# One transformer layer: a fixed issue order for the first units, chunk 2 turned by DMA, earlier mask constants, a new plan search

## The chip, the cores and the metric

The kernel runs on one core of a Trainium2 chip. A core has a matmul engine (TensorE, called PE in the profile; its weight loads appear as PEld), a vector engine (VectorE, DVE), a scalar engine (ScalarE, ACT), a general engine (GpSimd, POOL) and a sync engine (SyncE, SP) that mostly issues transfers (DMAs). Each engine runs its own instructions in the order of the program; between engines, semaphores order the work. The time is device microseconds for one execution of the whole kernel, with the median over several runs.

## The reference

The input x has 2048 tokens of 448 features, in bf16. A conditioning row c gives six rows of modulation, and two branches follow, each with a layer norm in front:

```
mod = (silu(c) @ w_mod)                      # six rows: sa, ca, ga, sb, cb, gb
h = layernorm(x) * (1 + ca) + sa
x = x + ga * A(h)
h = layernorm(x) * (1 + cb) + sb
x = x + gb * B(h)
```

A is attention with 16 heads of 28. A token attends to 8 keys: itself and those 2, 4, ... 14 positions back (keys before the start are masked out); its output goes through wo. B is a layer norm followed by an MLP: `gelu(y @ w1 + b1) @ w2 + b2`, with 1792 inner features.

## The kernel before

**Tiling.** Even and odd tokens are stored apart, so that a window with dilation 2 becomes a contiguous window of 8 within 1024 tokens. The 2048 tokens are 16 blocks of 128 (b or t in the code). Four blocks make a chunk, so there are chunks 0 to 3.

**Stages.** `front_ln(bs)` does the first layer norm for a list of blocks: per block a bn_stats and bn_aggr on VectorE (`stats`, L621), the reciprocal deviation on ScalarE (`rstd_act`, L626, an Ln and an Exp) for chunks 0 and 1 or on GpSimd (`rstd_pool`, L636) for 2 and 3, then a normalized block z on VectorE (`normalize`, L645). Then z must be turned, so that the features lie on the partitions, and the modulation (scale and bias per feature) is applied, which gives hT. There are two ways. For chunks in `TURN_PE` (L29) the matmul engine turns z with an identity matrix into PSUM (L757), and VectorE (L772) and ScalarE (L776) evict it, half each, with the modulation in the same instruction. For the other chunks SP issues a DMA transpose per block straight into hT (L781), and four VectorE instructions apply the modulation in place (L785). `front_qk(bs)` makes q and k from hT on PE (L705 and L712; the name pq), and ScalarE copies them out (L821). `values(b)` makes v (pv), ScalarE copies it (L854) and a DMA moves part of it to other partitions (L857). Chunk 0 goes through `front_ln` and `front_qk` in two units of two blocks, [0, 1] and [2, 3]; the other chunks go whole.

`attention(b)` handles one of nine groups: scores on PE (lt, L925), exp on ScalarE (et, L935), the mask on VectorE (L943), sums and values on PE (pd L957, po L965), Ln and Exp of the sums on ScalarE (den), and the division on VectorE (L991). `out_proj(t)` multiplies with wo (pw, L1006), adds to x (L1010), does the second and third layer norms on VectorE and turns the result y by DMA into yT (L1032). `mlp(j)` does four blocks of the MLP: w1 products (L705, L712, the name p), gelu on ScalarE (L1063), w2 products (L1076), the final addition (L1084) and the store. These come in three phases: attention 0 to 4 and MLP tile 0; attention 5, 6 and tile 1; attention 7, 8 and tiles 2, 3. Work for chunks 1, 2 and 3 is added behind attention 0, 2 and 3.

**What sets the order.** The code does not issue anything directly: every step is a task given to a planner (`add`) with its engine, an assumed duration, what it reads and writes, and the buffers it needs. The planner simulates the engines, picks among ready tasks the one of the highest rank, and searches: it disturbs the ranks at random for `TURNS` turns, the first `WIDE` of them widely and with a backward pass that recomputes ranks from the schedule, and keeps the order with the lowest mean cost over `DRAWS` replays with randomly longer tasks (`SLOW`). Two things bind the search. `rank_add` raises a task's rank. `seq` gives tasks of one engine a fixed order among themselves (`keep_sequences`, L131). The rank at the start (L153) includes `rank_add`; a backward pass (L155) computes ranks without it. PE idle time before 12 us is filled with warm-up matmuls (dummy, L613; L615), in a number proportional to `FILL_SHARE`.

**Loads.** The first loads stand in one list on SP: x of blocks 0 and 1, the modulation weights (wm_st), q and k weights, x of 2 and 3, v weights, x of 4 to 7; then `load_early` brings x of 8 to 11, the other modulation weights, x of 12 to 15, wo and b2. GpSimd memsets wo's tile to zero first (L538), since wo is loaded into it with gaps. GpSimd tasks given through `pool` are either free at once (`gated=False`) or held behind a gate (`pool_late`, L566), which follows the spreading of the q and k weights (`spread`, L790, L799).

Of the kernel before, what the change touches and what calls it, by code (L numbers as in the profile page):

```python
# [25 lines left out]
LEAD, SEP = 8, 8  # L26
WQ, WK, WE = 57, 64, 58
HL, HTW = 64, 592
TURN_PE = (0, 1, 2)  # L29
VENG = "SP"  # L30
SBQ, NSB, NBT = 2 * WQ, 18, 9
SBE = 4 * WE
# [4 lines left out]
DEN_SCALE = 2.0 ** -32  # L37
EXP_SET = "natural_log_exp_and_others"
START, NOISE, WINDOW = 0.8, (0.3, 1.0, 3.0), 3.4133
SEED, TURNS, WIDE = 15, 1500, 60  # L40
QKG = {256: ((0,), (1,), (2,), (3,)), 512: ((0,), (1,), (2,), (3,))}
W1G = ((0,), (1,), (2,), (3,), (4,), (5,), (6,))
SPREAD = ("DVE", "DVE")
# [4 lines left out]
]  # L48
FRONTS = (0, 2, 3)
LMM, DMM = 0.59, 1.0  # L50
FILL_UNTIL, FILL_SHARE = 12.0, 1.0
ROOM = {"S": 8, "et": 2, "den": 2, "zh": 6, "zb": 5, "T": 4, "hm": 4, "vb": 3, "vs": 2, "xp": 6}
DMA_RATE, TR_BYTES = 340e3, 480e3
SWITCH, SAME = 0.095, 1.0
FLEX = ("F", "64x128")
SEM = 0.07
DRAWS = 6
SLOW = {"BW": (0.5, 2.0), "SP": (0.1, 0.0), "PE": (0.0, 0.0), "any": (0.08, 0.0)}
DRAIN = {"PE": 0.165, "DVE": 0.085, "ACT": 0.105, "POOL": 0.05, "SP": 0.0, "BW": 0.0}


# [24 lines left out]
class Planner:  # L86
# [60 lines left out]
    def ranks(self):  # L147
        for t in reversed(self.sorted_tasks()):
            tail = 0.0
            for a in t.after:  # L150
                lag = (DRAIN[t.eng] + SEM + t.late) if a.before[t] else 0.0
                tail = max(tail, a.rank + lag)
            t.rank = t.us + tail + t.rank_add  # L153

    def backward(self):  # L155

# [17 lines left out]
    def forward(self):  # L174
# [13 lines left out]
        while len(order) < len(self.tasks):  # L188
            started = False
            for e in ("PE", "DVE", "ACT", "POOL", "SP", "BW"):  # L190
                if free_at[e] > now:
                    continue
                best, best_key = None, None
                shared = e in port and port["DVE" if e == "POOL" else "POOL"] > now
                for t in ready[e]:
                    if ready_at[t] > now or (shared and t.port):
                        continue
                    key = (-ready_at[t], -t.n) if e == 'BW' else (t.rank + ((SAME if t.mode == mode or t.mode == "flex" and mode in FLEX else 0.5 * SAME if t.mode != "F" and mode not in FLEX else 0.0) if e == "PE" else 0.0), -t.n)
                    if best is not None and key < best_key:
                        continue  # L200
                    need = {}
                    for b in t.bufs:
                        if b.slot is None:
                            need[b.room] = need.get(b.room, 0) + 1
                    if all(sum(x <= now for x in room[r]) >= n for r, n in need.items()):
                        best, best_key = t, key
                if best is None:
                    continue
                t = best
                t.fill = 0  # L210
                if e == "PE" and now < FILL_UNTIL:
                    t.fill = int(max(0.0, now - free_at[e]) * FILL_SHARE / (0.43 if now < 6.8 else 0.215))
                ready[e].remove(t)
                order.append(t)
                t.start = now
                started = True
                for b in t.bufs:
                    if b.slot is None:
                        b.slot = min(range(ROOM[b.room]), key=lambda k: room[b.room][k])
                        room[b.room][b.slot] = 1e9  # L220
                end = now + t.us
                if e == "PE" and t.mode == "flex":
                    t.closing = mode != "F"
                    end += 0.0 if mode in FLEX else SWITCH
                    mode = "F" if t.closing else "64x128"
                elif e == "PE" and t.mode != mode:
                    end += SWITCH
                    mode = t.mode
                free_at[e] = end
                t.cost = end - now  # L230
                if t.port:
                    port[e] = end
                done = end + DRAIN[e] + t.late
                for b in t.bufs:
                    users_left[b] -= 1
                    if users_left[b] == 0:
                        room[b.room][b.slot] = done + SEM
                for a in t.after:
                    left[a] -= 1
                    at = done + SEM if a.before[t] else end  # L240
                    if a.eng == e == "PE" or (a.eng == e and not a.before[t]):
                        at = end
                    ready_at[a] = max(ready_at[a], at)
                    if left[a] == 0:
                        ready[a.eng].append(a)
            if started:
                continue
            times = [v for v in free_at.values() if v > now] + [v for r in room.values() for v in r if now < v < 1e9]
            times += [ready_at[t] for e in ready for t in ready[e] if ready_at[t] > now]
            if not times:  # L250
                return None, 1e9
            now = min(times)
# [125 lines left out]
def kernel(  # L378
# [156 lines left out]

    late_pool = []
    b2_bc = sb("zh", [128, D], BF16, "b2_bc")
    add("POOL", 1.6, lambda: nc.gpsimd.memset(wo_s[:], 0.0), writes=["wo"], rank_add=440)  # L538

    def early(fn, nbytes, writes, reads=(), bufs=()):  # L540
        t, u = dma("SP", 0.5, fn, nbytes, writes, reads, bufs, chain["head"])
# [14 lines left out]
    def load_mlp(behind):  # L556
        chain["behind"] = behind
        for kt in range(KT):
            bulk(lambda kt=kt: nc.sync.dma_start(out=w1_s[:, kt], in_=B_w1[KOFF[kt]:KOFF[kt] + 128]), F * 256, [f"w1{kt}"],
                 lambda kt=kt: w1_s[0:1, kt, 0:1])  # L560
        for i in range(4):
            f0, f1 = 4 * i, min(4 * i + 4, FT)
            bulk(lambda f0=f0, f1=f1: nc.sync.dma_start(
                out=w2_s[:, f0:f1], in_=B_w2[128 * f0:128 * f1].rearrange("(ft p) n -> p ft n", p=128)),
                (f1 - f0) * 256 * D, [f"w2l{f // 2}" for f in range(f0, f1, 2)], lambda f0=f0: w2_s[0:1, f0, 0:1])

    def pool_late():
        gate = add("POOL", 0.1, lambda: nc.gpsimd.memset(wqk_st.t[0:1, 1, KT - 1, D - 8:D], 0.0), bufs=[wqk_st],
# [21 lines left out]
    def mask_rows():  # L590
        nc.gpsimd.memset(mask1[:], 1.0)
        for j in range(2):
# [3 lines left out]
            nc.gpsimd.affine_select(out=m, in_=m, pattern=[[-1, WE]], compare_op=ALU.is_ge, fill=0.0,  # L596
                                    base=0, channel_multiplier=1)

    pool(0.8, mask_rows, ["mask1"])
    pool(0.9, lambda: nc.gpsimd.tensor_copy(out=mask[:], in_=mask1[:].unsqueeze(1).to_broadcast([128, 16, WE])), ["mask"],  # L600
         ["mask1"])

    def consts():
        for vk in vkeys:
# [1 line left out]
        nc.gpsimd.memset(ones_k[:], 1.0)  # L606
        nc.gpsimd.memset(ones_k[0:WIN - 1, 1, :], 0.0)

    pool(0.9, consts, ["ones", "vpad"])

    pwm = ps_one([128, 512], "pwm")

# [6 lines left out]


    def stats(src, key, sl, mv, b):  # L621
        first = mv is mv1 and b < 4
        add("DVE", 0.53, lambda: nc.vector.bn_stats(out=st_all[:, sl, :], in_=src()), reads=key, writes=[f"st{sl}"], seq=b + 20 * (b > 1) if first else None)  # L623
        return add("DVE", 0.09, lambda: nc.vector.bn_aggr(out=mv[:, b, :], in_=st_all[:, sl, :]), reads=[f"st{sl}"],
                   writes=[f"mv{id(mv)}_{b}"], seq=2 + b + 20 * (b > 1) if first else None)

    def rstd_act(mv, which, b0, n, ra=0.0):
        ks = [f"mv{id(mv)}_{b}" for b in range(b0, b0 + n)]
        add("ACT", 0.2, lambda: nc.scalar.activation(out=tv_all[:, which, b0:b0 + n], in_=mv[:, b0:b0 + n, 1],
                                                     func=ACT.Ln, bias=eps_col[:]),  # L630
            reads=ks + ["eps"], writes=[f"tv{which}_{b0}"], after=[tbl0], seq=3 if b0 == 0 else None)
        add("ACT", 0.15, lambda: nc.scalar.activation(out=rs_all[:, which, b0:b0 + n], in_=tv_all[:, which, b0:b0 + n],
                                                      func=ACT.Exp, scale=-0.5),
            reads=[f"tv{which}_{b0}"], writes=[f"rs{which}_{b}" for b in range(b0, b0 + n)], seq=4 if b0 == 0 else None)

    def rstd_pool(mv, which, b0, n):  # L636
        ks = [f"mv{id(mv)}_{b}" for b in range(b0, b0 + n)]
# [89 lines left out]
    def front_ln(bs):  # L727
        ch = bs[0] // 4
        early = ch in TURN_PE
        if ch not in h_of:  # L730
            h_of[ch] = sb("T", [128, KT, HTW], BF16, "hT")
        hc = h_of[ch]
        for b in bs:
            stats(lambda b=b: x_all[:, b, :], [f"x{b}"], b, mv1, b)
        if ch <= 1:
# [13 lines left out]
        if early:  # L749
# [15 lines left out]
            for half, eng in enumerate(("DVE", "ACT")):  # L765
                ptr = ptrs[half]
                for k in range(2):
# [3 lines left out]
                    if eng == "DVE":  # L771
                        add("DVE", 0.07 + n / 800, lambda kt=kt, k=k, ptr=ptr, scale=scale, bias=bias: nc.vector.tensor_scalar(  # L772
                            out=hc.t[:, kt, o:o + n], in0=ptr.t[:, k, :], scalar1=scale, scalar2=bias,
                            op0=ALU.mult, op1=ALU.add), reads=["sa", "ca"], writes=w, bufs=[ptr, hc], seq=12 + 2 * kt + 20 * (bs[0] > 1) if bs[0] < 4 else None)
                    else:
                        add("ACT", 0.32 + n / 1400, lambda kt=kt, k=k, ptr=ptr, scale=scale, bias=bias: nc.scalar.activation(  # L776
                            out=hc.t[:, kt, o:o + n], in_=ptr.t[:, k, :], func=ACT.Identity, scale=scale, bias=bias),
                            reads=["sa", "ca"], writes=w, bufs=[ptr, hc], seq=8 - kt if 0 in bs else None)
            return
        for b in bs:  # L780
            dma("SP", 1.25, lambda b=b: nc.sync.dma_start_transpose(out=hc.t[:, :, HL + b % 4 * 128:HL + b % 4 * 128 + 128], in_=zs[b].t[:]),  # L781
# [20 lines left out]
    def front_qk(bs):  # L802
# [3 lines left out]
        for mps in QKG[n]:  # L806
# [11 lines left out]
            for m, p in zip([2 * mp + i for mp in mps for i in range(2)], bufs):  # L818
                dst = (qT if m < 4 else kT)[:, m % 4, c0:c0 + n]
                w = [f"{'q' if m < 4 else 'k'}{m % 4}_{b}" for b in bs]  # L820
                add("ACT", 0.06 + n / 1200, lambda dst=dst, p=p: nc.scalar.copy(out=dst, in_=p.t[:]), bufs=[p], writes=w)  # L821

    def h_edges(ch):
        hc = h_of[ch]
# [354 lines left out]
```

## Time and profile before

| what | value |
|---|---|
| runs | 11, median 176.86 us, from 175.4 to 177.96 |
| profiled execution | 175.97 us, of which the span from first to last instruction is 174.3 us |
| first projection of q (L705, pq) starts | 9.92 us |
| first MLP product (p<-yT,w_s) starts | 69.5 us |
| last matmul ends | 171.34 us |
| transposes on PE (L757) | 48, from 6.45 to 37.6 us |
| DMA transposes for hT (L781) | 4, from 29.4 to 42.8 us |

A row of the timeline gives the start, the length, the engine, the line of the code, the operation, the result and what it is made of, the count of instructions merged in it, and in brackets the idle time ahead of it and what ended that. An engine with "q" behind its name is that engine's instruction queue, for example SPq issuing a transfer. Ends of matmuls are modelled by the profiler, so neighbouring rows can overlap by a few tenths. The weight tile w_s stands for w1 and w2, since the profile leaves numbers out.

### The profile page before, as it was taken

What the parts mean: (1) busy time and instruction counts of PE and PEld (TensorE: products, weight loads), DVE (VectorE), ACT (ScalarE), POOL (GpSimd) and SP (SyncE); (2) the same over time, 40 slices, a digit from 0 to 9 for tenths busy, and PEclk for the clock granted to TensorE, in tenths of its full rate; (3) what the DMA queues carried; (4) which work ended last, traced back from release to release, by engine and by line L of the source; (5) the groups of instructions that cost most, each with busy time, mean ns of one, the idle gap of its engine ahead of it and who ended that gap; (6) DMA issues with size and microseconds to landing.
All of it is one profiled execution on the core that took longest, in us unless ns stands there. A gap on an engine that the chain in (4) does not pass through costs nothing.

```text
span 174.3 us, 5056 instructions
## 1 busy us (share of the span) xinstructions
PE 165.8 (95%) x2093; PEld 82.4 (47%) x2110; DVE 116.5 (67%) x325; ACT 110.1 (63%) x199; POOL 46.6 (27%) x85
## 2 busy tenths in 40 slices
PE   7897999999999999999999999999999999999993
PEld 2464554554444545334555433555443555334562
DVE  2589957589999999993374899783779882001121
ACT  2158878899759988577867686956946400685000
POOL 5034004231382444161230233432213462000000
PEclk9999999999999999999999999999999999999999
DMA  5999983314199914004111100431001133000111
GB/s 150 271 361 270 259 167 115 62 29 98 26 335 257 268 38 90 2 4 92 30 56 34 30 4 0 90 88 56 0 4 32 25 88 83 4 0 0 53 53 53
DMA packets 22421, 16.01 MB, mean 92 GB/s; under 512 B 11961, under 2 KB 21182, under 8 KB 22398
## 3 DMA queue, kind: packets, MB, share of 16 engines
q1 hardware_dynamic: 22388, 15.69, 35.1%
q8 instruction: 16, 0.26, 0.6%
q14 instruction: 7, 0.06, 0.1%
q10 hardware_dynamic: 10, 0.00, 0.0%
HBM read 10.05 MB, written 1.84 MB: 68 GB/s over the span
## 4 chain that ended last, share of the span: by engine, by line
PE 88%; ACT 5%; DMA 3%; issue 1%; SPq 1%; DVE 0%
PE p L1076 25%; PE p L705 21%; PE pq L705 11%; PE pw L1006 7%; PE pv L705 6%; PE p L712 4%; DMA wm_st<-in_w_mod_dram 3%; PE pq L712 3%; PE po L965 3%; PE lt L925 3%; ACT et L935 2%; PE pd L957 1%; PE pv L712 1%; ACT hT L776 1%; ACT vkeys L854 1%
## 5 line engine op out<-in xcount | busy, mean ns | idle before, releaser
L1063 ACT ACTIVATE hm<-p,b_col 128x512 bf16<-128x512 f32 x56 | 35.1, 685 | 26.2 <-PE p L712 23.2
L1076 PE MATMUL p<-w_s,hm 128*128 128x448 bf16 (+1 forms) x238 | 44.1, 342 | 0.0
L705 PE MATMUL p<-yT,w_s 128*128 128x512 bf16 x160 | 39.2, 380 | 0.7 <-issue 0.5
L1084 DVE TENSOR_TENSOR x_all<-p,x1p 128x448 bf16<-128x448 f32 (+1 forms) x17 | 10.1, 596 | 34.8 <-PE p L1076 34.8
L641 POOL TENSOR_TENSOR rs_all<-tv_all,neg_half 128x1 f32<-128x1 f32 (+1 forms) x34 | 20.9, 631 | 41.5 <-DVE tv_all L638 41.4
L1076 PEld LDWEIGHTS <-hm 128*128 128x128 bf16 x238 | 22.7, 98 | 18.7 <-issue 0.2
L1036 POOL TENSOR_TENSOR x1p<-x_all,gbb_bc 128x448 f32<-128x448 bf16 x16 | 18.7, 1168 | 46.8 <-DVE x_all L1010 17.3
L705 PEld LDWEIGHTS <-w_s 128*128 128x128 bf16 x168 | 15.2, 98 | 21.8 <-issue 5.9
L705 PE MATMUL pq<-hT,Wqk 128*128 128x512 bf16 (+1 forms) x112 | 22.4, 334 | 2.2 <-issue 1.0
L623 DVE BATCH_NORM_STATS2 st_all<-x_all 128x6 f32<-128x448 bf16 x32 | 18.8, 614 | 5.0 <-DMA x_all<-in_A_x_dram 5.0
L935 ACT ACTIVATE et<-lt 128x464 bf16<-128x464 f32 x36 | 17.5, 571 | 1.9 <-PE lt L925 1.8
L705 PEld LDWEIGHTS <-Wqk 128*128 128x128 bf16 x120 | 10.9, 98 | 11.7 <-issue 2.8
L1006 PE MATMUL pw<-wo_s,oT 128*128 128x448 bf16 x64 | 14.1, 353 | 0.0
L943 DVE TENSOR_TENSOR et<-et,mask 128x928 bf16<-128x928 bf16 x18 | 13.1, 755 | 1.4 <-ACT et L935 1.4
L646 DVE TENSOR_SCALAR z<-x_all,mv,rs_all 128x512 bf16<-128x512 bf16 (+1 forms) x32 | 12.5, 418 | 1.7 <-POOL rs_all L641 1.7
L991 DVE TENSOR_TENSOR oT<-po,den 128x456 bf16<-128x456 f32 x18 | 10.8, 626 | 3.9 <-ACT den L981 3.9
L821 ACT CAST qT<-pq 128x512 bf16<-128x512 f32 (+1 forms) x20 | 9.2, 516 | 5.1 <-PE pq L712 3.5
L978 ACT ACTIVATE den<-pd 128x464 f32<-128x464 f32 x18 | 9.1, 562 | 5.1 <-PE pd L957 5.1
L1010 DVE TENSOR_TENSOR x_all<-pw,x_all 128x448 bf16<-128x448 f32 x16 | 9.9, 617 | 3.4 <-PE pw L1006 3.3
L705 PE MATMUL pv<-Wv,hT 128*128 128x448 bf16 x54 | 11.4, 353 | 0.0
L821 ACT CAST kT<-pq 128x512 bf16<-128x512 f32 (+1 forms) x20 | 9.1, 510 | 2.6 <-PE pq L712 2.0
L854 ACT CAST vkeys<-pv 128x448 bf16<-128x448 f32 x18 | 8.8, 534 | 1.7 <-PE pv L712 1.0
(87 smaller groups left out, 184.2 us busy)
## 6 DMA issues: line engine op xcount, KB each, us to landing
w_s<-in_B_w_dram SPq DMA_DIRECT2D x7, 448.0 KB, 4.2
wmod<-in_w_mod_dram SPq DMA_DIRECT2D x4, 392.0 KB
out_dram<-x_all SPq DMA_DIRECT2D x7, 224.0 KB, 2.3
x_all<-in_A_x_dram SPq DMA_DIRECT2D x3, 448.0 KB, 7.0
vb<-vkeys SPq DMA_DIRECT2D x9, 128.0 KB
wqk_st<-in_A_wqkv_dram SPq DMA_DIRECT2D x4, 226.0 KB
wm_st<-in_w_mod_dram SPq DMA_DIRECT2D x2, 392.0 KB, 5.9
x_all<-in_A_x_dram SPq DMA_DIRECT2D x2, 224.0 KB
```

The source lines that it names most:

```text
L623: add("DVE", 0.53, lambda: nc.vector.bn_stats(out=st_all[:, sl, :], in_=src()), reads=key, writes=[f"st{sl}"], seq=b + 20 * (b > 1) if fir ...
L641: lambda: nc.gpsimd.tensor_tensor(out=rs_all[:, which, b0:b0 + n], in0=tv_all[:, which, b0:b0 + n], in1=neg_half[:, 0:n], op=ALU.pow),
L646: return add("DVE", us, lambda: nc.vector.tensor_scalar(out=dst(), in0=src(), scalar1=mv[:, b, 0:1], scalar2=rs_all[:, which, b:b + 1], op ...
L705: nc.tensor.matmul(outs[i].t[:], lhsT=w(i, kt, slice(0, 128)), rhs=x(i, kt, slice(0, 128)), start=(n == 0 and not last), stop=(n == 2 and ...
L712: nc.tensor.matmul(outs[i].t[:], lhsT=w(i, kt, rows), rhs=x(i, kt, rows), start=not last, stop=last, tile_position=(r0, 0))
L821: add("ACT", 0.06 + n / 1200, lambda dst=dst, p=p: nc.scalar.copy(out=dst, in_=p.t[:]), bufs=[p], writes=w)
L935: ex = add("ACT", 0.45, lambda r=r: nc.scalar.activation(out=et.t[:, r].rearrange("p n ft c -> p (n ft c)"), in_=lts[r].t[:].rearrange("p ...
L943: nc.vector.tensor_tensor(out=ev, in0=ev, in1=mask[:], op=ALU.mult)
L1006: nc.tensor.matmul(pw.t[:], lhsT=oT[:, ft, c0:c0 + 128], rhs=wo_s[:, ft, :], start=(ft == 0), stop=(ft == 3))
L1036: P.wrote(add("POOL", 1.05, lambda: nc.gpsimd.tensor_tensor(out=xp.t[:], in0=x_all[:, t, :], in1=gbb2_bc[:], op=ALU.add), reads=[f"x{t}", ...
L1063: gl = add("ACT", 0.57, lambda f=f, p=p: nc.scalar.activation(out=hm_at(f), in_=p.t[:], func=ACT.Gelu_apprx_tanh, bias=b1_col[:, f:f + 1]) ...
L1076: nc.tensor.matmul(p2.t[:], lhsT=hm_at(f)[:, bi * 128:(bi + 1) * 128], rhs=w2_s[:, f, c0:c1], start=(f == 0), stop=(f == FT - 1))
```

## The change

It has five parts.

1. **Fixed order.** `stats` now gives the bn_stats of blocks 0 to 7, rather than 0 to 3, a place in VectorE's sequence; those of 4 to 7 get 34 to 37, behind the normalization of blocks 2 and 3 (30 and 31). The Ln and Exp of blocks 2 and 3 get places 13.5 and 13.6 on ScalarE, between the copies of q (10 to 13) and k (14 to 17) of blocks 0 and 1, which also get places. The VectorE eviction of the turned blocks 2 and 3 loses its place. All tasks of `front_ln([2, 3])` are raised by `BOOST`, 6.
2. **Turning.** `TURN_PE` is (0, 1), so that chunk 2 goes the way of chunk 3.
3. **GpSimd.** The mask, its copy and the constants are no longer gated and have high ranks; the memset of wo's tile becomes a gated task.
4. **Ranks.** `rank_add` no longer enters the stored rank (and with it that of the tasks in front); it is added when a ready task is picked, after a backward pass too.
5. **Search.** Another seed, 1400 turns with 400 wide ones for 1500 with 60, smaller assumed delays of transfers, and warm-up matmuls for 0.75 of the idle time.

```diff
-TURN_PE = (0, 1, 2)
+TURN_PE = (0, 1)
...
-SEED, TURNS, WIDE = 15, 1500, 60
+SEED, TURNS, WIDE = 3, 1400, 400
...
-FILL_UNTIL, FILL_SHARE = 12.0, 1.0
+FILL_UNTIL, FILL_SHARE = 12.0, 0.75
...
-SLOW = {"BW": (0.5, 2.0), "SP": (0.1, 0.0), "PE": (0.0, 0.0), "any": (0.08, 0.0)}
+BOOST = 6.0
+SLOW = {"BW": (0.3, 1.2), "SP": (0.1, 0.0), "PE": (0.0, 0.0), "any": (0.06, 0.0)}
...
-            t.rank = t.us + tail + t.rank_add
+            t.rank = t.us + tail
...
-                    key = ... else (t.rank + ((SAME if ...
+                    key = ... else (t.rank + t.rank_add + ((SAME if ...
...
-    add("POOL", 1.6, lambda: nc.gpsimd.memset(wo_s[:], 0.0), writes=["wo"], rank_add=440)
...
+    pool(1.6, lambda: nc.gpsimd.memset(wo_s[:], 0.0), ["wo"])
...
-    pool(0.8, mask_rows, ["mask1"])
+    pool(0.8, mask_rows, ["mask1"], gated=False, rank_add=700)
...
-         ["mask1"])
+         ["mask1"], gated=False, rank_add=690)
...
-    pool(0.9, consts, ["ones", "vpad"])
+    pool(0.9, consts, ["ones", "vpad"], gated=False, rank_add=680)
...
-        first = mv is mv1 and b < 4
-        add("DVE", 0.53, ... seq=b + 20 * (b > 1) if first else None)
+        first = mv is mv1 and b < 8
+        add("DVE", 0.53, ... seq=b + 20 * (b > 1) + 10 * (b > 3) if first else None)
         return add("DVE", 0.09, ...
-                   ... seq=2 + b + 20 * (b > 1) if first else None)
+                   ... seq=2 + b + 20 * (b > 1) if first and b < 4 else None)
...
-            (Ln) ... seq=3 if b0 == 0 else None)
+            (Ln) ... seq={0: 3, 2: 13.5}.get(b0) if which == 0 else None)
-            (Exp) ... seq=4 if b0 == 0 else None)
+            (Exp) ... seq={0: 4, 2: 13.6}.get(b0) if which == 0 else None)
...
-            (eviction of ptr on DVE) ... seq=12 + 2 * kt + 20 * (bs[0] > 1) if bs[0] < 4 else None)
+            (eviction of ptr on DVE) ... seq=12 + 2 * kt if 0 in bs else None)
...
+            if bs[0] == 2:
+                for t in P.tasks[n0:]:
+                    t.rank_add += BOOST
...
-                add("ACT", 0.06 + n / 1200, ... nc.scalar.copy(out=dst, in_=p.t[:]), bufs=[p], writes=w)
+                add("ACT", 0.06 + n / 1200, ... nc.scalar.copy(out=dst, in_=p.t[:]), bufs=[p], writes=w,
+                    seq=10 + m if 0 in bs else None)
```

More of the change, by code (lines that the diff above doesn't have):

```diff
@@ L197, in forward @@
                         continue
-                    key = (-ready_at[t], -t.n) if e == 'BW' else (t.rank + ((SAME if t.mode == mode or t.mode == "flex" and mode in FLEX else 0.5 * SAME if t.mode != "F" and mode not in FLEX else 0.0) if e == "PE" else 0.0), -t.n)
+                    key = (-ready_at[t], -t.n) if e == 'BW' else (t.rank + t.rank_add + ((SAME if t.mode == mode or t.mode == "flex" and mode in FLEX else 0.5 * SAME if t.mode != "F" and mode not in FLEX else 0.0) if e == "PE" else 0.0), -t.n)
                     if best is not None and key < best_key:
@@ L621, in stats @@
     def stats(src, key, sl, mv, b):
-        first = mv is mv1 and b < 4
-        add("DVE", 0.53, lambda: nc.vector.bn_stats(out=st_all[:, sl, :], in_=src()), reads=key, writes=[f"st{sl}"], seq=b + 20 * (b > 1) if first else None)
+        first = mv is mv1 and b < 8
+        add("DVE", 0.53, lambda: nc.vector.bn_stats(out=st_all[:, sl, :], in_=src()), reads=key, writes=[f"st{sl}"], seq=b + 20 * (b > 1) + 10 * (b > 3) if first else None)
         return add("DVE", 0.09, lambda: nc.vector.bn_aggr(out=mv[:, b, :], in_=st_all[:, sl, :]), reads=[f"st{sl}"],
-                   writes=[f"mv{id(mv)}_{b}"], seq=2 + b + 20 * (b > 1) if first else None)
+                   writes=[f"mv{id(mv)}_{b}"], seq=2 + b + 20 * (b > 1) if first and b < 4 else None)
     def rstd_act(mv, which, b0, n, ra=0.0):
@@ L630, in rstd_act @@
                                                      func=ACT.Ln, bias=eps_col[:]),
-            reads=ks + ["eps"], writes=[f"tv{which}_{b0}"], after=[tbl0], seq=3 if b0 == 0 else None)
+            reads=ks + ["eps"], writes=[f"tv{which}_{b0}"], after=[tbl0], seq={0: 3, 2: 13.5}.get(b0) if which == 0 else None)
         add("ACT", 0.15, lambda: nc.scalar.activation(out=rs_all[:, which, b0:b0 + n], in_=tv_all[:, which, b0:b0 + n],
                                                       func=ACT.Exp, scale=-0.5),
-            reads=[f"tv{which}_{b0}"], writes=[f"rs{which}_{b}" for b in range(b0, b0 + n)], seq=4 if b0 == 0 else None)
+            reads=[f"tv{which}_{b0}"], writes=[f"rs{which}_{b}" for b in range(b0, b0 + n)], seq={0: 4, 2: 13.6}.get(b0) if which == 0 else None)
     def rstd_pool(mv, which, b0, n):
@@ L732, in front_ln @@
         hc = h_of[ch]
+        n0 = len(P.tasks)
         for b in bs:
@@ L773, in front_ln @@
                             out=hc.t[:, kt, o:o + n], in0=ptr.t[:, k, :], scalar1=scale, scalar2=bias,
-                            op0=ALU.mult, op1=ALU.add), reads=["sa", "ca"], writes=w, bufs=[ptr, hc], seq=12 + 2 * kt + 20 * (bs[0] > 1) if bs[0] < 4 else None)
+                            op0=ALU.mult, op1=ALU.add), reads=["sa", "ca"], writes=w, bufs=[ptr, hc], seq=12 + 2 * kt if 0 in bs else None)
                     else:
@@ L820, in front_qk @@
                 w = [f"{'q' if m < 4 else 'k'}{m % 4}_{b}" for b in bs]
-                add("ACT", 0.06 + n / 1200, lambda dst=dst, p=p: nc.scalar.copy(out=dst, in_=p.t[:]), bufs=[p], writes=w)
+                add("ACT", 0.06 + n / 1200, lambda dst=dst, p=p: nc.scalar.copy(out=dst, in_=p.t[:]), bufs=[p], writes=w,
+                    seq=10 + m if 0 in bs else None)
     def h_edges(ch):
```

## The prediction

> **What bounds the kernel now.** I read the page's busy rows first, then the chain of waits, then the stages one by one.
>
> The first two sections of the page:
>
> ```profile
> span 174.3 us, 5056 instructions
> PE 165.8 (95%) x2093; PEld 82.4 (47%) x2110; DVE 116.5 (67%) x325; ACT 110.1 (63%) x199; POOL 46.6 (27%) x85
> ...
> PE   7897999999999999999999999999999999999993
> ...
> DVE  2589957589999999993374899783779882001121
> ACT  2158878899759988577867686956946400685000
> ...
> DMA  5999983314199914004111100431001133000111
> ```
>
> Each digit is 4.36 us. TensorE (PE) has 174.3 - 165.8 = 8.5 us of idle in the whole span, so no scheduling change can win more than that unless it also takes work off PE. The table by stages says where those 8.5 us lie (columns: length, then busy time and count of PE, PEld, DVE, ACT, POOL, then clock, DMA share, GB/s):
>
> ```profile
> 16.00:18.00 2.00, 0.87 (x9) 0.51 (x10) 2.00 (x9) 2.00 (x5) 0.00 (x0) 1.00 1.07 263
> ...
> 34.00:36.00 2.00, 1.95 (x34) 1.24 (x23) 0.50 (x1) 2.00 (x6) 0.00 (x0) 1.00 0.33 66
> 36.00:38.00 2.00, 1.93 (x16) 0.79 (x15) 2.00 (x4) 2.00 (x5) 1.31 (x1) 1.00 0.00 0
> 38.00:40.00 2.00, 1.61 (x124) 1.44 (x124) 2.00 (x6) 1.97 (x5) 0.00 (x0) 1.00 0.03 8
> ...
> 50.00:60.00 10.00, 9.79 (x238) 4.88 (x238) 9.73 (x30) 7.87 (x17) 3.68 (x6) 1.00 1.08 290
> 60.00:70.00 10.00, 9.74 (x125) 4.72 (x126) 9.86 (x29) 8.50 (x14) 5.14 (x7) 1.00 0.40 63
> ```
>
> About 3.0 us are the tail after the last matmul (the last matmul ends at 171.34; the last rows are then added and stored), 2.2 us are the start before 10 us, where the modulation weights are awaited, and no edit is aimed at either. What is left is one hole at 16 to 18 us (1.13 us), some 0.7 us at 34 to 42, and small gaps, most of them 0.16 us wherever the matmul shape switches. So I expect a gain of about one per cent at best, from the first 42 us. The hole at 16 us in the timeline (start, length, engine, line, result, count, wait):
>
> ```profile
> 13.50 1.68 DVE L623 BATCH_NORM_STATS2 st_all<-x_all 128x6 f32<-128x448 bf16 x3 [0.92 <-DMA x_all<-in_A_x_dram]
> ...
> 15.18 0.70 DVE L646 TENSOR_SCALAR z<-x_all,mv,rs_all 128x512 bf16<-128x512 bf16 x2
> ...
> 15.62 0.83 PE L757 MATMUL ptr<-ident,z 128*128 128x128 bf16 x8
> ...
> 17.31 0.28 PE L705 MATMUL pq<-hT,Wqk 128*128 128x256 bf16 x1 [0.86 <-DVE hT L772]
> ```
>
> The reader is to see that z of blocks 2 and 3 comes at 15.18, although their rstd (Ln at 13.27, Exp from 14.13 for 0.22) was done by 14.35: VectorE was in three bn_stats of blocks 4 to 6. PE turned z at 15.62 and then had nothing until hT was written.
>
> The second place, 33.5 to 40 us:
>
> ```profile
> 36.17 1.49 ACT L776 ACTIVATE hT<-ptr,mod_col 128x512 bf16<-128x512 bf16 x2
> ```
>
> Here ScalarE works without a break from 34 to 42 us, and part of it is this eviction of the turned chunk 2. PE turns chunk 2 in two groups of eight matmuls, at 34.09 and 37.01, and stalls for 0.19 us at 38 and 0.27 us before 39.62, the latter behind ScalarE's den.
>
> **What the Trainium skill says.** "DMA: Bandwidth & Descriptors", DMA Transpose (X-bar): a plain DMA transpose is issued from SP or ACT only, and cannot compute on the way. The trace agrees: chunk 3, already turned so, has four transposes on SP (1.20 to 1.83 us each) and four VectorE affines after them (L785, 0.41 us). "VectorE: DVE Perf Modes", Why PSUM operands drop a tier: an operand in PSUM costs a faster mode. Here 128x512 from PSUM takes 0.53 us (L772), from SBUF 0.41 us. "TensorE: Matmul & The Clock Gate", What's actually happening: the array runs at half clock until a window of some 3.4 us has been busy, and the window runs free. The warm-up matmuls agree: six in 2.74 us (457 ns each) at 1.3 us, seven in 1.67 us (239 ns each) at 8.4 us. The clock row shows 1.0 throughout, so it does not show this.
>
> **The change, part by part**, against the profiled execution of 175.97 us (span 174.3 and 1.7 around it).
>
> First units of blocks 2 to 7. The bn_stats of blocks 4 to 7 are now placed behind both z of blocks 2 and 3. Stats and aggregate of 2 and 3 end at 12.59 as before. Their Ln and Exp (0.31 + 0.22 us) are fixed between the q and the k copies, so they run at about 12.7 to 13.2 instead of 13.27 to 14.35. z then comes at 13.3 to 14.0 rather than 15.18 to 15.88, so 1.9 us earlier; PE turns it ahead of or behind the first value product (13.40 to 14.9) and hT is written by about 15.9, while PE still has the scores (0.70 us to 15.6) and the transposes (0.45 us). The waits of 0.86 and 0.27 us go: -1.1 us. What is late next are the k copies, 0.5 us behind the Ln and Exp, which the scores at 14.92 need; they were done at 14.25, so that is hidden. Bounds 0 (hT waits for ScalarE behind the value copies) and -1.1.
>
> Chunk 2 turned by DMA. Off PE go 16 transposes: the next instruction follows 0.45 us after the first eight start (34.09 to 34.54) and 0.55 us after the second (37.01 to 37.56), -1.0 us. Off ScalarE go 1.49 us in a stretch where it is full, off VectorE 2 x 0.53; onto VectorE come 4 x 0.41, net +0.6 us; onto SP four issues of 1.2 to 1.8 us. Is h of chunk 2 in time? Five z are written by 30.3. Four issues at 1.5 us from 29.4 end at 35.4, the last lands about 2.5 us after its start (that of yT<-y), 36.4; affines until 38.1. Before, the last part of h was written at 40.15. The PE work ahead of it shrinks by 1.1 + 1.0, so PE could ask at 38.0: about level. The small stalls at 38 and 39.6 (0.19 + 0.27) should partly go with the emptier ScalarE: -0.2. I give back +0.2 for a short wait for h. Bounds: -1.5 (all stalls of the stretch go) and +2 (h late, second rival). The transposes run where the DMA share is 0.0 to 0.4, so nothing is crowded there.
>
> Warm-up share 0.75 for 1.0. Of seven dummies at 8.41 to 10.08 about five stay, ending at 9.6; the first projection could start when hT is written, 9.82, rather than at 10.08 by the chain: -0.1. Cover gone: were PE at half clock for one more window of 3.4 us, the projections from 9.9 would lose half of it, +1.7. In 1.3 to 6 us PE still has the bulk of its dummies, so I take -0.1.
>
> Masks ahead of the loads, wo memset behind them. The mask was ready at 15.17 and first used at 18.51, so nothing; the memset of 1.60 us now falls after the gate at 11.37, beside VectorE work, and the wo loads start at 17.31 behind other issues: nothing (bounds 0 to +0.3, if the shared port slows VectorE).
>
> New search. From 42 to 171 us PE is a full queue with 1.3 us of gaps, mostly shape switches. A new order can win perhaps 0.3 and lose more. I take +0.1, bounds -0.5 to +1.0.
>
> Sum: -1.1 - 1.0 - 0.2 + 0.2 - 0.1 + 0.1 = -2.1, so 173.9 for an execution like the profiled one. The median of the runs before, 176.86, lies 0.9 above it; on that base 174.8.
>
> **Rivals.** The gain is swallowed later (0.17). VectorE is 97% busy from 50 to 70 us, and its work on x begins only after the broadcast of the modulation rows lands at 30.4, which waits for loads that do not come earlier. The fourth transpose for the first MLP tile is issued at 64.85 and lands at about 67.4; PE uses it at 69.5, 2.1 us later. A PE that arrives 2.1 us earlier has used this slack, and VectorE's extra 0.6 us makes it wait. Against it: seven scalings of w2 (0.6 us each) stand in that stretch and most of them can move behind. It would leave 0 to 0.8 us of gain: 176.4.
>
> Slower by late transposes (0.22). SP issues in order. If chunk 2's transposes stand behind bounce copies of values (L857 waited 8.8 us for PE in all) or behind each other's z, h of chunk 2 comes late and PE runs out of first-chunk projections. It decides once h is complete more than 2 us after the 38.0 where PE asks; at 3.5 us late the sum is -2.1 + 3.5 = +1.4: 178.3. For it: the page's 34 to 42 us has almost no spare work. Against it: chunk 3 went this way with 4 us in hand.
>
> A better plan than I count (0.10): all of the gaps at 34 to 42 and half of those later, -3.3: 173.6.
>
> **How the numbers follow.** My forecast, 174.8, has 0.51, its own range 174.0 to 175.8. About 0.5% (0.9 us) is what a measurement can tell from no change. Faster: 0.51 + 0.10 = 0.61; no change: 0.17; slower: 0.22. To leave out no more than 2 in 10 the range takes in the swallowed case and the edge of the slow one: 173.2 to 177.8.
>
> **What would show it.** Right: bn_stats of blocks 4 to 6 after two z on VectorE; no wait on hT at L705 before 18 us; 32 transposes at L757, eight DMA transposes at L781; ScalarE with idle at 34 to 42; the first MLP product about 2 us before 69.5. Wrong: a PE wait of a microsecond on hT of chunk 2 at 36 to 42, one on yT near 68, or 256-wide matmuls at over 200 ns apart after 10 us.

## The result, and the profile after

The changed kernel takes 174.14 us (median of 12 runs, 173.34 to 174.85), and the kernel before 176.87 (47 runs). The ratio is 0.9856, 95% interval 0.9831 to 0.988: faster by 1.4%, or 2.5 us. The ratios leave out executions more than 1.5% above the fastest of their kernel, so they can differ a little from the quotient of two medians. The profiled execution took 174.73 us, 1.2 below that of the kernel before (175.97). The two profiles therefore show about half of what the medians show. The whole gain of the profile is there at the first MLP product, which starts at 68.17 for 69.52.

The first two sections of the page of the changed kernel:

```profile
span 173.0 us, 5023 instructions
PE 164.8 (95%) x2073; PEld 81.9 (47%) x2088; DVE 116.2 (67%) x327; ACT 108.3 (63%) x197; POOL 48.6 (28%) x85
...
PE   7699999999999999999999999999999999999993
...
DVE  3575999699899999994554788896689922100121
ACT  3237989789887969669677954768938300475200
```

PE is busy for 1.0 us less; the busy time of the transposes alone goes from 3.7 to 2.7 us. Its idle time is 173.0 - 164.8 = 8.2 us by the page, hardly below the 8.5 of before. About 1.5 us of both numbers are no idle time but matmuls that the record lacks (see the new search below). The table by stages, its columns as before:

```profile
16.00:18.00 2.00, 1.64 (x77) 1.28 (x76) 1.01 (x3) 1.57 (x4) 0.00 (x0) 1.00 1.08 267
...
34.00:36.00 2.00, 2.00 (x12) 1.00 (x11) 1.99 (x6) 2.00 (x5) 0.00 (x0) 1.00 0.60 118
36.00:38.00 2.00, 2.00 (x72) 1.05 (x72) 2.00 (x6) 1.14 (x4) 1.23 (x1) 1.00 0.44 89
38.00:40.00 2.00, 1.84 (x11) 0.94 (x11) 1.68 (x6) 2.00 (x5) 1.42 (x2) 1.00 0.67 114
```

The hole at 16 us has shrunk from 1.13 to 0.36 us, and ScalarE, full at 36 to 38 us before, is idle for 0.86 us there. But the start of the timeline has something that the plan does not want:

```profile
8.28 2.34 PE L617 MATMUL pwm<-warm_w 128*128 128x512 bf16 x5 [0.24 <-issue]
...
10.41 1.49 PE L707 MATMUL pq<-hT,Wqk 128*128 128x256 bf16 x6
...
14.10 0.73 DVE L648 TENSOR_SCALAR z<-x_all,mv,rs_all 128x512 bf16<-128x512 bf16 x2 [2.00 <-ACT rs_all L634]
...
14.75 1.14 DVE L625 BATCH_NORM_STATS2 st_all<-x_all 128x6 f32<-128x448 bf16 x2
...
16.32 0.62 PE L760 MATMUL ptr<-ident,z 128*128 128x128 bf16 x8
...
17.94 0.29 PE L714 MATMUL pq<-hT,Wqk 64*128 64x256 bf16 x2 [0.36 <-ACT hT L779]
```

VectorE's order is the one that the change fixes: both z of blocks 2 and 3, then the bn_stats of block 4 on. Yet the warm-up matmuls take 468 ns each and the first six projections 1.49 us, where before they took 239 ns and 0.82 us: with fewer warm-up matmuls the array is still at half clock, though the clock column shows 1.00 here. The fixed order passes the delay on. ScalarE's Ln for blocks 2 and 3 stands behind the copies of q, so it runs at 13.53 us, where the prediction had 12.7; VectorE waits 2.00 us for it and starts z at 14.10 instead of 13.3. So the projections of blocks 2 and 3 start at 17.94, no sooner than before (one at 17.31, the rest from 17.86), and the gain of the profile comes later.

### The profile page after: what moved, and what is told of

The parts are those of the page before. It is cut to its first block, busy times and chain, and to the rows that moved or that the text cites. A ratio compares the mean times of both kernels' runs of the same rounds, so it can differ in the third digit from the quotient of the medians.

```text
span 173.0 us, 5023 instructions
## 1 busy us (share of the span) xinstructions
PE 164.8 (95%) x2073; PEld 81.9 (47%) x2088; DVE 116.2 (67%) x327; ACT 108.3 (63%) x197; POOL 48.6 (28%) x85
## 4 chain that ended last, share of the span: by engine, by line
PE 89%; ACT 4%; DMA 3%; issue 1%; DVE 1%; ACTq 0%; SPq 0%
PE p L1083 25%; PE p L707 21%; PE pq L707 11%; PE pw L1013 7%; PE pv L707 6%; PE p L714 4%; PE lt L932 3%; PE pq L714 3%; DMA wm_st<-in_w_mod_dram 3%; PE po L972 2%; PE pwm L617 2%; PE pv L714 1%; ACT hT L779 1%; PE pd L964 1%; ACT kT L827 1%
## 5 line engine op out<-in xcount | busy, mean ns | idle before, releaser
L643 POOL TENSOR_TENSOR rs_all<-tv_all,neg_half 128x1 f32<-128x1 f32 (+1 forms) x34 | 23.1, 688 | 50.6 <-DVE tv_all L640 44.2
L950 DVE TENSOR_TENSOR et<-et,mask 128x928 bf16<-128x928 bf16 x18 | 14.2, 796 | 1.2 <-ACT et L942 1.2
```

What stands on the lines that cost most here:

```text
L643: lambda: nc.gpsimd.tensor_tensor(out=rs_all[:, which, b0:b0 + n], in0=tv_all[:, which, b0:b0 + n], in1=neg_half[:, 0:n], op=ALU.pow),
L950: nc.vector.tensor_tensor(out=ev, in0=ev, in1=mask[:], op=ALU.mult)
```

## The experiments

Each run stood beside runs of the kernel before on the same chip. The ratio to those is what is compared, since the median of the kernel before moved from 176.3 to 177.5 us between the three groups of runs. From a_turn012 on, a percentage against the changed kernel is taken from its second measurement, a_again (0.9865).

**Warm-up share back to 1.0 in the changed kernel (a_fill1).**

```diff
-FILL_UNTIL, FILL_SHARE = 12.0, 0.75
+FILL_UNTIL, FILL_SHARE = 12.0, 1.0
```

> The changed kernel with the warm-up share put back to 1.0: six more warm-up matmuls before 10 us, every other instruction in the same order. In the profile of the changed kernel the array is still at half clock from 8.3 to 12.4 us (warm-up matmuls 468 ns each, the first 256-wide projections 248 ns apart), where the kernel before was at full clock by 8.4. Theory W (the smaller share costs 1.4 us there): this one is 0.7 to 1.5 us faster than the changed kernel in the median, 172.6 to 173.4, and its profile has projections under 120 ns apart from 10 us. Rival (the window runs free, so the moment of warming is chance, and the six matmuls only stand in the way): same as the changed kernel within 0.4 us, 173.7 to 174.5.

Measured: 175.02 us, ratio 0.9871 (0.9814 to 0.9928), where the changed kernel had 0.9856. The array is warm, and nothing is won. PE's timeline shows why:

```profile
7.75 1.67 PE L617 MATMUL pwm<-warm_w 128*128 128x512 bf16 x7
9.26 0.82 PE L707 MATMUL pq<-hT,Wqk 128*128 128x256 bf16 x6
...
15.88 0.28 PE L714 MATMUL pq<-hT,Wqk 64*128 64x256 bf16 x2 [0.36 <-ACT hT L779]
...
20.03 0.76 PE L877 MATMUL pb<-wmod,silu_bc 112*32 112x448 bf16 x10
22.09 0.56 PE L877 MATMUL pb<-wmod,silu_bc 112*32 112x448 bf16 x6 [1.30 <-DMA wmod<-in_w_mod_dram]
```

and the same product in the changed kernel:

```profile
22.09 0.94 PE L877 MATMUL pb<-wmod,silu_bc 112*32 112x448 bf16 x16
```

The projections of blocks 2 and 3 come at 15.88, 2.1 us sooner than in the changed kernel. Then PE comes to the modulation product at 20.03, waits 1.30 us for its last weights to land at 22.09, and passes it at 22.65. The changed kernel, with its cold start, reaches that product at 22.09 without a wait and passes it at 23.03. Theory W falls: the cold array costs 2 us at 16 us and 0.4 at 23. The load of the modulation weights is what PE waits for in this stretch. The 0.4 us are gone a little later: VectorE, with the eviction of chunk 1 behind a bn_stats in its order, waits for the load of x until 24.88 (the changed kernel runs that bn_stats at 24.06), and PE waits for hT of chunk 1.

```profile
24.88 0.63 DVE L625 BATCH_NORM_STATS2 st_all<-x_all 128x6 f32<-128x448 bf16 x1 [2.98 <-DMA x_all<-in_A_x_dram]
25.42 0.98 DVE L775 TENSOR_SCALAR hT<-ptr,mod_col 128x512 bf16<-128x512 bf16 x2
```

The first MLP product then starts at 68.60, 0.4 us behind the changed kernel.

**The share of 0.75 in the kernel before (b_fill75).**

```diff
-FILL_UNTIL, FILL_SHARE = 12.0, 1.0
+FILL_UNTIL, FILL_SHARE = 12.0, 0.75
```

> The kernel before with the warm-up share at 0.75, nothing else changed. Theory W: slower than the kernel before by 0.7 to 1.5 us. Rival (chance): same within 0.4 us. A third reading, that fewer warm-up matmuls let the first projections start sooner, as the prediction had it: faster by 0.1 to 0.2.

Measured: 177.68 us, ratio 1.0018 (0.9986 to 1.0049): the same. Here too the warm-up matmuls were at 468 ns at 8.5 us in the profile. No effect of the share shows, in either kernel.

**One edit in the finished order of the kernel before (b_moved).** The bn_stats and bn_aggr of block 4 on are taken from ahead of the z and evictions of blocks 2 and 3 and put right behind them.

```diff
     P.plan()
+    move = [i for i, (t, f, c) in enumerate(P.order) if t in late_stats]
+    last = max(i for i, (t, f, c) in enumerate(P.order) if t in early_z)
+    keep = [e for i, e in enumerate(P.order) if i not in move or i > last]
+    at = 1 + max(i for i, (t, f, c) in enumerate(keep) if t in early_z)
+    P.order = keep[:at] + [P.order[i] for i in move if i < last] + keep[at:]
     P.emit()
```

> The kernel before, its plan found as before, and then one edit by hand in the finished order: the bn_stats and bn_aggr of block 4 and later that stood on VectorE ahead of the z and the evictions of blocks 2 and 3 are put right behind those evictions. Theory H (the hole of 1.1 us at 16 to 18 is made by these instructions, and what is won there lasts to the end): 0.7 to 1.1 us faster, and the profile shows at L705 no wait of more than 0.3 us on hT before 19 us. Rival (what is won is lost again later in the fixed order, since the rest waits for loads): within 0.4 us of the kernel before, with new waits on PE between 20 and 45 us.

Measured: 178.71 us, ratio 1.0103 (1.0072 to 1.0133): slower by 1%, which neither theory had. VectorE starts z at 14.25 now, but the two take 1.19 us for 0.70, while GpSimd copies the mask beside the first of them (13.93 to 14.89). That the copy hinders it fits the Trainium skill, "GPSIMD Engine Reference", Specifications (GpSimd's SBUF interfaces are shared with VectorE, which matters for some of VectorE's instructions); in the kernel before, two bn_stats ran beside the same copy at their usual 0.61 us. It was not tried by itself. More important, the hole stays, 1.40 us for 1.13:

```profile
15.42 0.62 PE L765 MATMUL ptr<-ident,z 128*128 128x128 bf16 x8
16.55 0.28 PE L713 MATMUL pq<-hT,Wqk 128*128 128x256 bf16 x1 [0.51 <-DVE hT L780]
17.73 0.89 PE L713 MATMUL pq<-hT,Wqk 128*128 128x256 bf16 x5 [0.89 <-ACT hT L786]
```

PE's own order has the turning behind the scores, and ScalarE's order has its half of hT behind two exps. The second wait, 0.27 us when it was hidden behind VectorE, is now 0.89. And the Ln of chunk 1, which needs the moved statistics, runs at 19.97, where it had run at 18.10. So VectorE's order is not all that keeps the hole open. In the changed kernel the turning (16.32) stands ahead of the scores, and ScalarE's half of hT ahead of the exps. The clock fell in this profiled execution, as in 4 of the 22, but those 4 were not the slower ones (178.20 us, the others 178.87).

**Chunk 2 turned by DMA, all else as before (b_turn01).**

```diff
-TURN_PE = (0, 1, 2)
+TURN_PE = (0, 1)
```

> The kernel before with chunk 2 turned by DMA and nothing else changed (the old settings of the search, so the plan is a new one). Theory T (the 16 transposes taken off PE are worth their 1.0 us, ScalarE's relief 0.2): 0.8 to 1.5 us faster, first MLP product at about 68.5. Rival S (the gain of the change is the search's luck, and each new plan is a new draw): anywhere from 1 us faster to 1 us slower, with PE idle before 70 us that has nothing to do with chunk 2. Rival L (h of chunk 2 comes late, as in the prediction's slower case): slower, with a wait of over 1 us at the chunk 2 projections.

Measured: 177.5 us, ratio 1.0005 (0.9977 to 1.0033). The profile has a new wait of 0.55 us on copies of k before 15.60 and one of 0.93 us on hT before 18.07 (0.86 and 0.27 in the kernel before). Neither has to do with chunk 2, and the granted clock (the column before the last two) falls behind the second of them:

```profile
16.00:17.00 1.00, 1.00 (x61) 0.75 (x32) 1.00 (x4) 1.00 (x4) 0.00 (x0) 1.00 1.13 289
17.00:18.00 1.00, 0.14 (x3) 0.00 (x0) 1.00 (x4) 1.00 (x4) 0.00 (x0) 0.85 1.04 270
18.00:19.00 1.00, 0.93 (x5) 0.68 (x6) 1.00 (x6) 1.00 (x3) 0.00 (x0) 0.50 1.06 283
19.00:20.00 1.00, 1.00 (x7) 0.18 (x5) 1.00 (x7) 0.45 (x2) 0.00 (x0) 0.50 1.04 136
20.00:21.00 1.00, 1.00 (x7) 0.72 (x6) 1.00 (x4) 0.92 (x5) 0.00 (x0) 0.50 1.09 266
21.00:22.00 1.00, 1.00 (x11) 0.68 (x10) 1.00 (x6) 0.61 (x2) 0.19 (x1) 0.95 1.09 261
```

The mean clock of an execution shows such a fall as about 0.99. It did so in 12 of the 22 executions here (median 178.41 us, the other ten 176.78), and in 11 of 59 of the kernel before beside them (177.88, the others 177.15). Where the clock stayed up, this plan was 0.4 us ahead, which ten executions do not secure; the falls took that back.

**Warm-up matmuls in the hole of the kernel before (b_busy).**

```diff
+            def project(closing, pairs=pairs, bs=bs):
+                if bs == [2, 3] and not kept_busy:
+                    kept_busy.append(True)
+                    for k in range(8):
+                        nc.tensor.matmul(pairs[0][0][0].t[:], lhsT=warm_w[:, 0:128], rhs=warm_w[:, 0:256], start=True, stop=True)
+                packed(pairs, closing)
```

> The kernel before, in its own order, with eight 256-wide warm-up matmuls (0.86 us at full clock) put on PE right ahead of the first projection of blocks 2 and 3. They go into the PSUM tile that the projection then overwrites and wait for nothing, so they lie in the hole of 1.1 us at 16 to 18 us. Theory K (the hole costs more than its width: in other executions of the unchanged order the granted clock fell to 0.50 for 3.4 us right after it, as the profiles of b_fill75, b_moved and b_turn01 showed, which costs 1.7 us each time it happens): the median falls by 0.7 to 1.4 us with no useful instruction moved, and the profile shows clock 1.00 from 16 to 24. Rival N (the clock's fall is seldom, or is hidden by loads that PE has to wait for anyway, the modulation weights at 22 us among them): within 0.4 us of the kernel before.

Measured: 176.72 us, ratio 1.0012 (0.997 to 1.0053). The eight matmuls lie where they should (16.18 to 17.22), and nothing is won: theory K falls as an explanation of the change. The mean clock shows a fall in 2 of 14 executions here and in 24 of 139 of the kernel before over all three groups. Those 24 had a median of 177.86 us, the others 176.78 (group by group the difference is 0.7, 1.5 and 0.8). So a fall costs about 1 us, but it is too rare in the kernel before to be the gain.

**The changed kernel with chunk 2 on PE (a_turn012).**

```diff
-TURN_PE = (0, 1)
+TURN_PE = (0, 1, 2)
```

> The changed kernel with chunk 2 turned on PE again, newly planned with the settings of the change. Theory T (the transposes off PE are worth their 1.0 us and ScalarE's relief): 0.8 to 1.5 us slower than the changed kernel, 174.9 to 175.6. Rival S (luck of the search): 173.5 to 177. If K is right and the hole is closed here too, it stays below 176.

Measured: 176.17 us, ratio 0.9984 (0.995 to 1.0017), 1.2% above the changed kernel. The profiled spans are 174.0 and 173.0 us, and the first MLP product starts at 69.2 and 68.2: the 1.0 us that the transposes take from PE. The other 1.1 us in the medians is not in the profiles. The plan is a new one too, so that the two numbers agree does not by itself show the cause.

**The changed kernel with the old fixed places (a_noseq).**

```diff
-        first = mv is mv1 and b < 8
+        first = mv is mv1 and b < 4
...
-seq={0: 3, 2: 13.5}.get(b0) if which == 0 else None
+seq=3 if b0 == 0 else None
...
-BOOST = 6.0
+BOOST = 0.0
```

> The changed kernel with the places in the sequences and the raise of blocks 2 and 3 as they were before (bn_stats of blocks 4 to 7 free, Ln and Exp of 2 and 3 free, the eviction of 2 and 3 fixed again), newly planned. Theory H and K (the fixed order closes the hole and keeps the clock): 1 to 2 us slower than the changed kernel, with a hole of about a microsecond on PE before the projections of blocks 2 and 3 and, in some executions, a clock of 0.5 behind it. Rival (the search closes the hole by itself, or the place where PE next waits is the load of the modulation weights at 22 us): within 0.5 us of the changed kernel.

Measured: 176.18 us, ratio 0.9965 (0.9937 to 0.9994), 1.0% above the changed kernel. The hole is 0.51 us only. PE's list of waits (total, times, longest) names another place:

```profile
PE p L707 <- DMA yT<-y: 1.2, 1, 1.2
...
PE pq L707 <- DVE hT L775: 0.5, 1, 0.5
PE pb L876 <- DMA wmod<-in_w_mod_dram: 0.5, 1, 0.5
```

PE waits for the modulation weights, and then 1.2 us for yT at the first MLP product (69.11). That is the place that the prediction's first rival named; this plan does what the rival said, the changed kernel's does not.

**The changed kernel with the old search (a_oldsearch).**

```diff
-SEED, TURNS, WIDE = 3, 1400, 400
+SEED, TURNS, WIDE = 15, 1500, 60
...
-            t.rank = t.us + tail
+            t.rank = t.us + tail + t.rank_add
```

> The changed kernel with the old search: seed 15, 1500 turns of which 60 wide, the old assumed delays, and rank_add in the stored rank again. Theory P (the tasks and the fixed places carry the gain): within 0.6 us of the changed kernel. Rival S (the new plan carries it): 1 us or more slower, 175.1 to 177, with PE idle or waits between 20 and 70 us that the changed kernel does not have.

Measured: 180.64 us, ratio 1.0218 (1.0156 to 1.0279), 3.6% above the changed kernel and 2.2% above the kernel before, with the same tasks and places as the changed kernel. Its profile has 1.33 us of PE idle from 40 to 50 us and a mean clock of 0.83 there.

**The changed kernel once more (a_again), the new search on the old tasks (b_search), and other seeds (a_seed4, a_seed7).** The edits, in this order: none; the settings of the search and the rank as in the change; the seed alone in the last two.

```diff
-SEED, TURNS, WIDE = 15, 1500, 60
+SEED, TURNS, WIDE = 3, 1400, 400
...
-            t.rank = t.us + tail + t.rank_add
+            t.rank = t.us + tail
```

> The changed kernel itself, as the measure for the other runs of this group. Its first measurement was 0.9856 of the kernel before (0.9831 to 0.988). Expected 0.984 to 0.989 again.

> The kernel before, its tasks and fixed places as they were, with the search of the change: seed 3, 1400 turns of which 400 wide, the smaller assumed delays, and rank_add at the moment of picking. Rival S in its strong form (the wider search alone brings the gain): 1 to 2 us faster than the kernel before. Theory P with luck (what the search finds depends on tasks, places and seed together, and a seed that suits one set of tasks means nothing for another): between 1 us faster and 2 us slower. The plan's own length, as the planner counts it, is 177.9 for this and 176.7 for the kernel before, so by its count it should be slower by up to 1.2.

> The changed kernel with seed 4 in place of 3 and nothing else. This measures how much the draw of the search is worth at the same tasks, places and settings. Theory S (a plan is a draw, and seed 3 is a good one): 1 to 2 us slower than the changed kernel; the planner counts a length of 175.85 for it and 173.79 for the changed kernel. Theory P (the parts carry it): within 0.5 us of the changed kernel.

> The changed kernel with seed 7, the one of seeds 3 to 8 with the lowest cost by the planner's own count (176.59 to 176.84 for seed 3; lengths 173.78 and 173.79). If the planner's count ranks plans as the chip does, this is within 0.5 us of the changed kernel, on either side; if its count says little about the chip, it can be 1 us or more slower.

Measured:

```
kernel      median   ratio    95% interval
a_again     174.76   0.9865   0.9811 to 0.9918
b_search    179.36   1.0134   1.0077 to 1.0191
a_seed4     178.20   1.0058   1.0024 to 1.0092
a_seed7     175.41   0.9909   0.9881 to 0.9937
```

With another seed, and not one other character changed, the kernel is 2.0% slower than the changed kernel (1.0058 / 0.9865) and slower than the kernel before. Two stages of a_seed4 tell where:

```profile
20.00:30.00 10.00, 8.30 (x142) 4.83 (x143) 8.61 (x29) 7.62 (x16) 2.14 (x3) 1.00 0.66 160
...
40.00:50.00 10.00, 8.16 (x158) 3.80 (x158) 7.50 (x22) 7.95 (x16) 0.63 (x1) 0.83 0.49 131
```

PE is idle for 1.7 us in the one and 1.8 us in the other, where the changed kernel has 0.24 and 0.53. In the second, the scores stall three times from 39.7 to 42.2 us, and the clock falls for some 3.4 us (10 us at 0.83 is 1.7 lost, at half clock): eleven projections take 4.45 us there and 2.54 in the changed kernel. The new search on the old tasks is worse than the old one, by 1.3%, so the wider search does not bring the gain alone; seed 7, which the planner ranked level with seed 3, comes within 0.5% of it. The planner's own count puts seeds 3 and 7 ahead of seed 4 and that ahead of b_search, as the chip does, but it also puts seed 4 ahead of the kernel before, which the chip does not. None of these versions beats the changed kernel.

## Why the prediction was right, and where it was not

**Direction and size.** It said 174.8 with 173.2 to 177.8, from a sum of -2.1 us; the medians give -2.5 by the ratio. That the number came so close is in good part luck. The sum was worked out for the profiled execution, and there it is -1.2 instead of -2.1: about 1.0 fits the length of the turning, and 0.3 is left for everything else, where the sum had 1.1 for the first units alone. The rest of the 2.5 us lies between the medians and the two profiles, one 0.9 us below its median, the other 0.6 above. The first MLP product came 1.35 us earlier, not the 2 that were given as a sign.

**Chunk 2 turned by DMA: -1.0, in agreement with the profiles, not shown by itself.** The transposes' busy time fell by 1.0 us, and a_turn012 stands 1.0 us behind at the first MLP product and at the end. But in b_turn01, another new plan, the same edit gained nothing in the median. The side conditions hold: eight transposes go out on SP in one row, and the modulation of chunk 2 ends at 36.96, before the predicted 38.1.

```profile
27.91 12.06 SPq L787 DMA_TRANSPOSE hT<-z  x8
...
36.55 0.41 DVE L791 TENSOR_SCALAR hT<-hT,mod_col 128x512 bf16<-128x512 bf16 x1
```

That is 1.5 us for each, as taken from chunk 3. They landed 3.3 to 4.2 us after their issue, not 2.5; h was in time because the first issue stood at 27.91 instead of 29.4. PE never waits for hT of chunk 2, and the slower rival did not come up in the changed kernel.

**First units: -1.1, the mechanism seen, the price wrong.** The hole went from 1.13 to 0.36 us. But the step "What is late next are the k copies" failed: what is late next is the load of the modulation weights. a_fill1 shows that 2 us won at 16 us are 0.4 at 23 us and nothing after the load of x. That an early part of a load-bound start is worth its width cannot be kept. b_moved shows a second error: the prediction put the hole down to VectorE, and the orders of PE and ScalarE take part in it. The prediction also put the 2.2 us before 10 us down to the modulation weights; 1.29 of them are the wait for the first warm-up tile (warm_w), 0.8 the weights.

**Warm-up share: -0.1, wrong in its mechanism.** The case named as "cover gone", one more window at half clock, did happen in the profile. It cost nothing that can be measured; in a_fill1 the waits for the loads take back what a warm array wins.

**Masks.** Nothing was taken for them, and no run tried them alone. The 1.19 us for two z in b_moved, against 0.73 in the changed kernel, hint at a use for an early mask copy; that is argued, not shown.

**New search: +0.1 with -0.5 to +1.0, the term that was mis-sized most.** With the tasks and places of the change, one seed against another makes 2.0% (3.5 us), and the old settings 3.6%. The bound came from PE's gaps after 42 us, that is from what a better plan could win; what a worse plan can lose has no such bound, since a stall of 2 us can take the clock along. And the gaps themselves, 1.3 us, were no idle time. The record of the kernel before has 2093 matmuls for 2110 weight loads, so matmuls are missing. The four profiles with as many matmuls as loads (b_busy, a_turn012, a_noseq, a_oldsearch) have none of the gaps of 0.16 us that the prediction read as shape switches; all others have some. PE from 42 to 171.34 us, first in the kernel before, then in b_busy, which has the same order:

```profile
42.00:171.34 129.34, 128.06 (x1499) 61.63 (x1509) 86.13 (x235) 80.44 (x134) 35.70 (x46) 1.00 0.25 64
...
42.00:171.34 129.34, 129.33 (x1511) 61.59 (x1509) 85.97 (x235) 80.42 (x133) 36.16 (x46) 1.00 0.26 64
```

PE is full there, and a better plan had no idle time to win behind 42 us. The draw is larger than any part of the change was reckoned to be.

**What stays open.** How much of the gain belongs to the fixed places cannot be told: a_noseq is 1.0% slower, but its plan is also a new draw, and its loss sits at yT. The measurements give only this: with the old tasks the new search is 1.3% slower than the old one, with the new tasks the old search is 3.6% slower than the new one (one seed in each, but three of the new search on the new tasks: 0.9865, 0.9909, 1.0058). Neither tasks nor search won by themselves, and how far the best of them is a lucky draw is open. And half of the difference of the medians is not in the profiled executions, of which the one of the kernel before was 0.9 us below its median.

## What to carry to other kernels

When a searched plan issues the work, measure several seeds of the old and of the new version before a part of an edit is credited: here the draw was worth 2% and the whole change 1.4%. Work taken off the engine that is full came out at its own length in one pair of plans and was lost again in another; time won ahead of a load that is awaited anyway was lost. Reordering one engine did not close a hole that other engines' orders held open too. And before small gaps on PE are counted as idle, the number of matmuls in the record is to be compared with the number of weight loads.

## What the hardware showed that was not expected

The clock of the array fell to 0.50 for some 3.4 us after a stretch of one or two microseconds with little PE work, and the matmuls behind it took up to twice as long (4.45 us for eleven instead of 2.54). In the kernel before it happened in 17% of the executions (24 of 139), in a_seed4 in 14 of 19, in b_turn01 in 12 of 22, in a_oldsearch in all 6, in the changed kernel in 1 of 18 over both of its measurements. The Trainium skill, "TensorE: Matmul & The Clock Gate", What's actually happening, gives half clock after an idle window of some 3.4 us; here PE was not idle for so long: in b_turn01 it was busy for 0.14 us of the one microsecond ahead of the fall, in a_seed4 the stalls ahead of it were 0.80, 0.27 and 0.91 us. What makes the fall likely is not settled: with the hole of the kernel before filled it still came in 2 of 14 executions, and where in them it lay is not known, since only the mean clock was kept for executions without a profile.
